# Sink keys and values in place of spent slots, merged casts and a new plan for all instructions, in a fused attention and SwiGLU kernel

## Chip, core and metric

The kernel runs on one core of a Trainium2 chip. The metric is the device time of one launch in microseconds (us), the median of several runs. A core has TensorE (PE, matmuls; PEld is its loading of weights), VectorE (DVE), ScalarE (ACT), GpSimd (POOL) and SyncE (SP, which here issues the DMA transfers). PE writes to PSUM banks; the other engines take results from there to SBUF.

## The reference, cut to what matters

Attention over 4 batches, 8 heads, 768 positions, head size 64, followed by a SwiGLU block on 3072 tokens of 512 features with 1536 inner features. Heads 0, 2 and 6 ("retrieval" heads) see all earlier positions. The other five ("streaming" heads) see the first four positions (the sinks) and the last 64.

```python
def _attn_ref(q, k, v, is_retrieval, n_sink, window):
    scores = scale * np.matmul(q, k.transpose(0, 1, 3, 2))
    rel = pos[:, None] - pos[None, :]
    causal = rel >= 0
    is_sink = pos[None, :] < int(n_sink)                  # n_sink = 4
    in_win = (rel >= 0) & (rel < int(window))             # window = 64
    stream_keep = causal & (is_sink | in_win)
    mask = np.where(retr, causal, stream_keep)
    scores = np.where(mask, scores, -1000000000.0)
    a = np.exp(scores - np.max(scores, axis=-1, keepdims=True))
    a = a / (np.sum(a, axis=-1, keepdims=True) + 1e-09)
    return np.matmul(a, v)

def _moe_ref(x, w_gate, w_val, w_out):
    g = x @ w_gate
    silu = g * (1.0 / (1.0 + np.exp(-g)))
    return silu * (x @ w_val) @ w_out
```

All inputs and the output are float32; the kernel computes in float16 with float32 sums.

## The kernel before

The positions of a batch are cut into six tiles of 128; tile `i` of a batch has queries and keys 128 i to 128 i + 127. Two tiles make a pair (`n`), which is the unit of loading: one DMA of 512 KB each for q, k and v (called x in the plan). Four tiles make a group (`g`) of 512 tokens, for which the SwiGLU block runs once over 12 slices (`j`) of 128 inner features. Everything that the kernel does is a task in a list; a string, ORDER, gives the order of the tasks in the program (two digits of base 62 for each task number; numbers from 3700 are that many plus 3700 dummy "warm" matmuls), and a string of digits, WAYS, says for each task on which of its possible engines it runs. The tile framework adds the semaphores, so each engine goes through its tasks in the given order and waits where an operand isn't ready.

```python
RINGS = {"raw": 11, "hq": 2, "e": 6, "xb": 3, "xt": 2, "sig": 2, "sil": 3, "ahead": 3,
         "h": 2 * NJ, "osb": 2, "gv": 3, "o": 1, "sc": 1, "av": 1, "tr": 1, "queue": 4}
PAIRS = [(0, 2), (4, 6), (1, 3), (5, 7)]      # two heads share the 128 rows of kT
kT = [const.tile([128, 4, S], FH, name=f"kT{n}") for n in range(2)]         # batch b uses b % 2
k2 = [const.tile([128, 4, 4, 128], FH, name=f"k2_{n}") for n in range(2)]
vt = [const.tile([128, NT, 8, 66], FH, name=f"vt{n}") for n in range(2)]
v2 = [const.tile([128, 4, 8, 66], FH, name=f"v2_{n}") for n in range(2)]
# ... cut ...
def mask_order():
    ps = buf("tr", [128, 4, 128], FP, "mk")       # the bank that transposes use as well
    nc.tensor.matmul(ps..., perm, nat..., start=True, stop=True)
def mask_fill(x):                                  # nine DVE instructions in two tasks
    ...
# ... cut ...
def cast(n, kd, j):                                # q or k of a pair, one half of the positions
    ...                                            # float32 raw -> float16 hq (or hqz)
def castv(n, m, j):
    copy(T_v[n, m][j], vt[b % 2][j * 64:(j + 1) * 64, 2 * pi + m, :, 0:64],
         r[m * 64:(m + 1) * 64, :, j])
# ... cut ...
def sinks_k(b):        # the sinks' keys into all four tiles of k2
    for j, ns in enumerate((NSINK - NSINK // 2, NSINK // 2)):
        copy(T_prev[b, 0][0], K2[:, :, :, j * 64:j * 64 + ns],
             T[:, :, j * 64:j * 64 + ns].unsqueeze(2).to_broadcast([128, 4, 4, ns]))
def sinks_v(b, m):     # the sinks' values into tile m - 1 of v2
    for j, ns in enumerate((NSINK - NSINK // 2, NSINK // 2)):
        copy(T_prev[b, 0][m], V2[j * 64:j * 64 + ns, m - 1], V[j * 64:j * 64 + ns, 0])
def previous_k(b, m):  # the last 64 keys of tile m
    copy(T_prev[b, m][0], K2[:, :, m - 1]...[:, :, :, 32:64], T[...][:, :, :, 32:64])
def previous_v(b, m):  # the last 64 values of tile m
    for r in (32, 96):
        copy(T_prev[b, m][1], V2[r:r + 32, m - 1], V[r:r + 32, m])
# ... cut ...
def block(t, p, kt):   # keys for a score matmul; kt < 0 means "sinks and the tile before"
    if kt < 0 and i > 1:
        return k2[b % 2][:, p, i - 2, :]
    kt = max(kt, 0)
    return kT[b % 2][:, p, kt * 128:(kt + 1) * 128]
def value(t, h, kt):
    if kt < 0 and i > 1:
        return v2[b % 2][:, i - 2, h, 0:65]
    return vt[b % 2][:, max(kt, 0), h, 0:65]
# ... cut ...
def gate(g, j, c, wsb, d):          # "gate" with wg_sb and "vals" with wv_sb: 4 matmuls each
    for kk in range(4):
        nc.tensor.matmul(ps, wsb[:, kk, j * 128:(j + 1) * 128], xt[:, kk, c[0]:c[1]], ...)
def outproj(g, tt, third):          # 4 matmuls of 512 columns; three of them for 128 tokens
    for j in range(third * 4, third * 4 + 4):
        nc.tensor.matmul(o_open[g, tt], hs[g, j][:, tt * 128:(tt + 1) * 128], wo_sb[:, j, :], ...)
```

A streaming head thus needs for tile `i` its own keys and a second tile of 128 slots, in which the four sinks and the last 64 keys of tile `i - 1` lie; the slots between are zero and masked. For `i` = 1 the tile before holds the sinks itself, so it is used as it is. Within a tile the positions are laid out as 64 even ones and then 64 odd ones, so the last 64 are slots 32 to 63 and 96 to 127.

Of the kernel before, what the change touches and what calls it, by code (L numbers as in the profile page):

```python
# [7 lines left out]
FP = mybir.dt.float32  # L8
# [8 lines left out]
    "000B010A0C0E0D0G0I030F050K2H0604xq070H2I090O2J2K020Jy52U2G080S2M2O2L2Vxu2P0L2W2Q2z0M2R2N3t0P302S"  # L17
    "0U312T3u32yQ2X0T372Y2Z383C0N2a392b2j1w0Q3D2l2k2e3E2m2f0Vxj2n5U2c0Y2d1x212p2g2o2r3A2q0R3B0m35342s"
    "xs2u2h2v3F3o3r2t2w0Z2i3p0c2x332y3G0n22xoBK10BU1y1z3H3PBL3I363qBM0d0oBN253JBXBVBO3Q3KBW115V3LxlBe"
    "3M0q3sBoBY3R3b0pBf0WBpBh28Bg3S3TBqBr3U3V3N0r230s3Oxi3W5QBs5S3X3Y5T0XBi3Z0u3d3a3eBP3c0tBZ5PBQBj0a"  # L20
    "3i5RBR3mBaBS3fBb0v3hBk3n0gBc3g24Bl3j4cBT3wBmBd4d0bBtBn0eBy4P3kBu3v4QC33l0hBzBv0i3x4SC0BwC40f4XBx"
    "3y0y27C1C50j4RC63z4Y1240C22BC80z41C7162ACDC9134Z43CA424514CI46CE174aCJ2DCF18CB44CK20154BCCCN0k4C"
    "4b26CG19CO4D0w2C4ECS0lCH4F1ACcCPCT0x4G4H4eCL2F1CCU29CQ4ICM1B1ECX2ECR4JCY4g4K1DCV4W4U1GCZ4V4TCdCW"
    "4h1FCa5C1I4f474iCb4j5D1H48Ce4k1K4LCf4m4l5E1JCiCg4n5H4M5K5I5J4q5L4oCj1L4p1M5G5M4w5F494r4xCkCh601O"
    "6F1N4sCl4z4A4yCoCm501P5N4t676252641Q5OCp65Cn1S5653514u1RCq6H574v54Cr4N1U66551TCuCs616q5863Cv5X1V"
    "5W591W6s4O5Y6t6v5ACw5Z5B6ECt1YD06r1X5a6u5bD1D57hCx6A5c1ZD26C5gD66D5e5dD37P5h5f6BD8CyD77Q7S7U705m"
    "CzDA7RD471686GD95nDF7j1a69DBDD7g5o1cDCDG5i1b5pDHDK6p1eDE5qDI7T1dDNDLDJ8T6o1g5j5sDy1f8E5rDM6w5t5k"
    "DODP8F5l1hDU8IDQ8JDS8HDRDV8G6x6I6yDZ6JDW5uDTDeDa6z8Q5v8VDXDbDf6L6KDj6MDg7O5w8O8RDk6ODYDc6PDlDh5x"
    "6NDdDo1i8PDi5y1kDpDt7N1j1m5z6QDmDuDq6RDv8UDr1lDn1o6YDw6ZDs1nDz1qDx6a6SE06T1p1s6bE16U6cE46V1rE26e"
    "6W6f6i6XE56j1t7Z6d6g94E67X9f6hE3E7727a6k957Y8S7iEA9i6l989p739k6mEB966n7B9j9hEM997CECE89q74A17E75"  # L30
    "ED7D9gE9EP7V7F76EG979r7W77EN9zEH78EO7HERAlEQ8DEI7IES8M9s7GEUETEJ7J7dA0EE8NEW7e7K7bEVEbAkEF79EX7f"
    "EZEYEc7c7A7LEeEdEaEg8C7M9EElEhEf7kEmEiEj7lEnEo9F8KEkEq7m8L1uEvErEp9G7sEsEwEt1vEx92F0Eu93F57tF19H"
    "EK7nF2F6Ey7oF7ELAYF3EzAa7pFAAW9yAgAX7qAZF87rFBF47yAn7uFCFDAb7zAhAiFFF98081FEFGFI827vFKFH7wAjFJ86"
    "FL83Am7x84FM879A85FN8W889C9B8XFQ898Z9DFR8Y8A8aFSFO8B9e8gFT8c8hFW9dFPFUFi8bFVFn8dFsFjFk8eFX8f8mFt"
    "8iFoFl8j8nFpFY8kFmFqFZFu8l8pFaFrFv8qFxFb8oFwFcFy8sFzG28r8tG7G3G0G88uG98w9l8vFdG18x9IFeG49n9m9J8y"
    "Ff9K9R9oGC9SFg8zG5GD9TFh90GAGEG6GH91GBAVAUGMGI9UGJGN9XAeGg9V9YGOGFAcAf9WGKGG9Z9t9w9uGPAdGL9aGh9v"
    "9xGQ9bGR9LGWGS9c9MGT9NGbGX9OGUGYGc9PGdGZGV9QA2GaGeA3H4GfA4A5H5GiA6H6AAH9GjABA7GkA8GmHAA9HBH7GlAC"
    "H8GnADAGAEGoAHHCGpAIAFAJGqGsAKHDAOGrGtALAPAMGuHEANGvHJGwHFGyHGHKGxHOHLAoHPHHApHQHMHIHTHNAQHUHRAR"
    "HVArASGzAsHSHWATAtH0HXAuAqHYAvH1AyHdHZAzH2HaAwI2AxHeH3B4HfB0B5HbB1B6B7B2HiB8HcBEB3HnHjBFB9HkBAHo"
    "HgBBHpHlHhBCHmI3BDBGHqBHHsBIHrHxHtBJHvHuHyI0HzHwIQI1IVIRITISIWIYIXIUI4IZIaI5IfI6IbIdIcIgI7IiIhIe"  # L40
    "I8IjIkIpIlIuImIqInIrIvIsIwIoIxItI9IyIzIAJ0J4J1IBJ9J5ICJOJ6JAJ2JBIDJ7J3JEJ8JJJFJCJGJKJHJLJDJMJIJP"
    "JNJQJRJUJSIEJVJTIFJWIGJXJaJYIHJbJZIIIKIJJcILJdJgJeIMJfJhINIOJiJjIPJkJl"
)
WAYS = (
    "000010000000000000000000000000000000000000000000000000000000000000000000000000000000000000000000"
    "000000000000000000000000211000010000000010111000001010011000000000000000000000000001000000200010"
    "000000010000000000000000000000011001101000001110110010010000000000100100100000000000000110110010"
    "110000010000000001001001000000000010001001000011001000010010000000000000000000000001100000200000"
    "000100001000000000000000000100000000010010011000000100100000000000000000012000022000000101001010"
    "001001000000000000010000000010002021000000000011001001000000000000000100000000000000010200000000"  # L50
    "001000000000001000000221011000000000011100100100100000000000001000000000002000021200000000101100"
    "100000000000000010000000000000000000000000000000000000000000000000000000000000000000000000000000"
    "000000000000000000000001000000000001000000000000000000000000000000000000000000000000000000000000"
    "000001000000000001000001000000000000000000000000000000000000000000000000000000000000000001000000"
    "000000000000000000000000000000000000000000000000000000000000000000000000000000000000000001000001"
    "000000000000000000000000000000000000000000000000000000000000000000000001000001000001000000000000"
    "00000000000000000000000000000000000000000000000000000100000100000100000000"
# [4 lines left out]
class Task:  # L62
# [3 lines left out]

    def __init__(self, name, ways, pos, run, deps=(), takes=(), kind="", after=(), grp=None):  # L70
        self.name, self.ways, self.pos, self.run = name, ways, pos, run
        self.deps, self.takes, self.kind = list(deps), list(takes), kind
        self.after = [x for x in after if x]
        self.grp = grp or name
        self.way = None


class Plan:
# [3 lines left out]

    INTO, BACK = 0.096, 0.120

    def __init__(self, rings):
        self.tasks = []
        self.rings = rings  # L90
        self.users = {}

    def add(self, *a, **k):
        t = Task(*a, **k)
        self.tasks.append(t)
        return t

# [4 lines left out]
    def order(self):  # L102
        n = len(self.tasks)
        numbers = [DIGITS.index(ORDER[2 * i]) * 62 + DIGITS.index(ORDER[2 * i + 1])
                   for i in range(len(ORDER) // 2)]
        assert sorted(x for x in numbers if x < 3700) == list(range(n)) and len(WAYS) == n
        for t, w in zip(self.tasks, WAYS):
            t.way = t.ways[int(w)]
        return numbers
# [3 lines left out]
def kernel(  # L113
# [22 lines left out]
    assert 0 < NSINK <= 64 and 0 < WIN <= 64  # L136
# [15 lines left out]
    QUARTERS = 0  # L152
# [9 lines left out]
    RINGS = {"raw": 11, "hq": 2, "e": 6, "xb": 3, "xt": 2, "sig": 2, "sil": 3, "ahead": 3,  # L162
             "h": 2 * NJ, "osb": 2, "gv": 3, "o": 1, "sc": 1, "av": 1, "tr": 1, "queue": 4}
# [17 lines left out]
    def copy(task, dst, src):  # L181
        if task.way[0] == "ACT":
            nc.scalar.copy(out=dst, in_=src)  # L183
        else:
            ENG[task.way[0]].tensor_copy(out=dst, in_=src)  # L185


    def act(n):
        return ("ACT", 0.083 + n * 0.000833, 0.225 + n * 0.000833, 0)

    def dve(d):
        return ("DVE", d - 0.05, d + 0.05, 0)

    def both(d):

        return ("DVE", d + 0.4, d + 0.45, 1)

    def pool(d):
        return ("POOL", d - 0.04, d + 0.06, 0)

    def pe(d):
        return ("PE", d, d + 0.22, 0)
# [32 lines left out]
    def make_masks():  # L235
        def keep(n, base, qstep, kstep):
            nc.gpsimd.affine_select(
                out=nat[:, n], in_=nat[:, n], compare_op=ALU.is_ge, fill=OFF, base=base,
                pattern=[[qstep, 2], [2 * qstep, 64]], channel_multiplier=kstep)

        nc.gpsimd.memset(perm, 0.0)
# [7 lines left out]
        keep(BAND0, 0, 1, -1)  # L249
        keep(OWN, WIN - 1, -1, 1)  # L250
# [7 lines left out]
    def mask_order():  # L258
        ps = buf("tr", [128, 4, 128], FP, "mk")
# [22 lines left out]
    k2 = [const.tile([128, 4, 4, 128], FH, name=f"k2_{n}") for n in range(2)]  # L282
    vt = [const.tile([128, NT, 8, 66], FH, name=f"vt{n}") for n in range(2)]
    v2 = [const.tile([128, 4, 8, 66], FH, name=f"v2_{n}") for n in range(2)]
# [10 lines left out]
    def fill2(x):  # L295
        ENG[T_fill2[x].way[0]].memset((k2[0], v2[0], k2[1], v2[1])[x], 0.0)

    warm_ps = []

    def warm(n=40):  # L300
# [3 lines left out]
        for _ in range(n):  # L304
            nc.tensor.matmul(warm_ps[0][:, 0:128], ident, ident, start=True, stop=True)

    T_masks = P.add("masks", [("POOL", 8.1, 8.1, 0)], -9.0, make_masks)
    T_fill0 = P.add("fill", [("DVE", 6.1, 6.1, 0)], -9.1, fill)
    T_fill1 = P.add("fill1", [("POOL", 0.35, 0.4, 0)], -8.9, fill1, after=[T_masks])
    T_fill2 = [P.add(f"fill2{x}", [dve(0.95), pool(1.7)], -0.5, (lambda x=x: fill2(x)),  # L310
                     after=[T_fill0]) for x in range(4)]
    T_mord = P.add("mord", [pe(0.216)], -0.5, mask_order, deps=[T_masks], takes=["tr"])
    T_fill = [P.add(f"mfill{x}", [dve(1.3 + 0.1 * x)], -0.4, (lambda x=x: mask_fill(x)),
# [28 lines left out]
    def whole(n):  # L342
        return [(kd, n) for kd in "qkx"]
# [698 lines left out]
```

The softmax here doesn't subtract the row's maximum and nothing guards it: scores larger than these inputs give would overflow.

## Time and profile before

| | |
|---|---|
| time, median of 3 (lowest, highest) | 268.44 us (268.37, 268.48) |
| span of the profiled execution | 266.5 us |
| instructions | 5265 |
| read from HBM, written | 28.31 MB, 6.29 MB |
| copies into v2 and k2, on POOL | 36 x 0.62 us, 7 x 0.40 us |
| copies into v2 and k2, on ACT | 28 x 0.63 us, 9 x 0.41 us, 8 x 0.22 us |
| casts of q and k to hq | ACT 28, DVE 5, POOL 1, of 512 elements |
| exponentials (e<-sc) | 71 on ACT, 62.2 us |
| tanh (sig<-gv) | 76 on ACT, 43.3 us |
| loads | 54 of 512 KB, all issued by SP |

How to read the lines: a row of digits gives the busy share in tenths for 40 equal slices of the span. A line of a group gives the line of the program, engine and operation, output and inputs by name with shape and type, how often (x), then busy us in all and mean ns of one, then the idle time of the engine just before and what ended it. The chain of waits is followed back from the last instruction to whatever released each step; "DMA" in it is the time from the issue of a transfer to its landing. An instruction in the timeline has its start, its length, and the idle time before it in brackets.

### The profile page before, as it was taken

What the parts mean: (1) busy time and instruction counts of PE and PEld (TensorE: products, weight loads), DVE (VectorE), ACT (ScalarE), POOL (GpSimd) and SP (SyncE); (2) the same over time, 40 slices, a digit from 0 to 9 for tenths busy, and PEclk for the clock granted to TensorE, in tenths of its full rate; (3) what the DMA queues carried; (4) which work ended last, traced back from release to release, by engine and by line L of the source; (5) the groups of instructions that cost most, each with busy time, mean ns of one, the idle gap of its engine ahead of it and who ended that gap; (6) DMA issues with size and microseconds to landing.
All of it is one profiled execution on the core that took longest, in us unless ns stands there. A gap on an engine that the chain in (4) does not pass through costs nothing.

```text
span 266.5 us, 5265 instructions
## 1 busy us (share of the span) xinstructions
PE 254.4 (95%) x1984; PEld 146.4 (55%) x1984; DVE 171.6 (64%) x345; ACT 171.0 (64%) x283; POOL 92.3 (35%) x126
## 2 busy tenths in 40 slices
PE   7899689999999999999999999999999999999993
PEld 7777565566555555654555555545555654444441
DVE  7665678867476886549876455578446767466332
ACT  3799999999999874895696555665443643423000
POOL 8748866445358323388003230520122020000000
PEclk9999999999999999999999999999999999999999
DMA  7999999999899939956543911551231200101134
GB/s 189 305 333 333 305 328 383 317 246 305 259 292 217 230 85 299 213 108 127 118 92 60 159 39 43 117 100 23 63 76 21 57 7 17 39 2 41 39 89 109
DMA packets 75193, 41.23 MB, mean 155 GB/s; under 512 B 27552, under 2 KB 70560, under 8 KB 75168
## 3 DMA queue, kind: packets, MB, share of 16 engines
q1 hardware_dynamic: 75088, 40.78, 61.6%
q8 instruction: 15, 0.25, 0.4%
q10 hardware_dynamic: 80, 0.13, 0.2%
q14 instruction: 10, 0.08, 0.1%
HBM read 28.31 MB, written 6.29 MB: 130 GB/s over the span
## 4 chain that ended last, share of the span: by engine, by line
PE 71%; ACT 17%; DMA 3%; SPq 3%; issue 2%; DVE 1%; ACTq 0%
PE gv L875 40%; PE o_ps L904 20%; PE sc L594 7%; ACT e L604 5%; ACT v L183 4%; PE av L624 4%; DMA raw<-in_v_dram 3%; ACT vt L183 2%; ACT hq L183 2%; SPq L330 2%; ACT sig L881 2%; SPq L338 1%; ACT k L183 1%; PE tr L472 1%; ACT wo_sb L183 0%
## 5 line engine op out<-in xcount | busy, mean ns | idle before, releaser
L604 ACT ACTIVATE e<-sc 128x1024 f16<-128x1024 f32 (+4 forms) x71 | 62.2, 880 | 26.3 <-PE sc L594 25.9
L875 PE MATMUL gv<-xt,wv_sb 128*128 128x512 f16 (+1 forms) x304 | 70.8, 368 | 1.3 <-DVE sil L885 1.3
L904 PE MATMUL o_ps<-wo_sb,h 128*128 128x512 f16 x288 | 71.2, 379 | 0.1
L875 PE MATMUL gv<-xt,wg_sb 128*128 128x512 f16 (+1 forms) x304 | 70.6, 368 | 0.6 <-DVE xt L185 0.5
L885 DVE SCALAR_TENSOR_TENSOR sil<-sig,gv 128x512 f32<-128x512 f32 (+1 forms) x76 | 49.7, 656 | 31.7 <-ACT sig L881 31.1
L881 ACT ACTIVATE sig<-gv 128x512 f32<-128x512 f32 (+1 forms) x76 | 43.3, 574 | 36.5 <-PE gv L875 36.2
L892 DVE SCALAR_TENSOR_TENSOR h<-sil,gv 128x512 f16<-128x512 f32 (+1 forms) x76 | 48.7, 654 | 7.7 <-PE gv L875 7.0
L612 POOL TENSOR_TENSOR e<-e,m 128x640 f16<-128x640 f16 (+1 forms) x16 | 27.5, 1716 | 69.4 <-ACT e L604 54.3
L875 PEld LDWEIGHTS <-wv_sb 128*128 128x128 f16 x304 | 28.9, 98 | 29.0 <-issue 2.0
L875 PEld LDWEIGHTS <-wg_sb 128*128 128x128 f16 x304 | 28.9, 98 | 27.9 <-issue 1.6
L904 PEld LDWEIGHTS <-h 128*128 128x128 f16 x288 | 26.8, 98 | 26.1 <-issue 0.5
L594 PE MATMUL sc<-qT,kT 128*128 128x256 f16 (+1 forms) x228 | 35.6, 257 | 1.3 <-ACT e L604 1.2
L594 PEld LDWEIGHTS <-kT 128*128 128x128 f16 x228 | 20.5, 98 | 12.8 <-issue 2.3
L624 PEld LDWEIGHTS <-e 128*128 128x128 f16 x472 | 20.1, 97 | 8.2 <-ACT e L604 0.9
L185 POOL COPY v<-vt 32x528 f16<-32x528 f16 (+1 forms) x36 | 22.4, 621 | 4.6 <-ACT vt L183 2.5
L185 POOL CAST vt<-raw 64x512 f16<-64x512 f32 x23 | 15.8, 689 | 20.9 <-DMA raw<-in_v_dram 16.3
L624 PE MATMUL av<-vt,e 128*128 128x65 f16 x392 | 21.8, 193 | 0.5 <-ACT e L604 0.4
L641 DVE TENSOR_TENSOR xb<-av,rc 128x256 f16<-128x256 f32 x47 | 19.8, 424 | 1.6
L629 DVE RECIPROCAL rc<-av 128x4 f32<-128x4 f32 x48 | 8.5, 178 | 19.0 <-PE av L624 18.7
L183 ACT CAST hq<-raw 128x512 f16<-128x512 f32 x28 | 16.9, 617 | 4.4 <-DMA raw<-in_q_dram 3.6
L185 DVE COPY o_sb<-o_ps 128x512 f32<-128x512 f32 x14 | 9.6, 688 | 14.4 <-PE o_ps L904 14.4
L612 DVE TENSOR_TENSOR e<-e,m 128x1024 f16<-128x1024 f16 (+1 forms) x22 | 14.7, 670 | 6.3 <-ACT e L604 6.2
(62 smaller groups left out, 193.7 us busy)
## 6 DMA issues: line engine op xcount, KB each, us to landing
raw<-in_q_dram SPq DMA_DIRECT2D x12, 512.0 KB, 7.1
raw<-in_k_dram SPq DMA_DIRECT2D x12, 512.0 KB, 7.0
raw<-in_v_dram SPq DMA_DIRECT2D x12, 512.0 KB, 6.6
out_dram<-o_sb SPq DMA_DIRECT2D x47, 128.0 KB, 2.4
raw<-in_moe_w_gate_dram SPq DMA_DIRECT2D x6, 512.0 KB, 7.8
raw<-in_moe_w_val_dram SPq DMA_DIRECT2D x6, 512.0 KB, 8.4
raw<-in_moe_w_out_dram SPq DMA_DIRECT2D x6, 512.0 KB, 8.6
kT<-hq SPq DMA_TRANSPOSE x16, 2.4
```

Source lines behind the costliest of these rows:

```text
L183: nc.scalar.copy(out=dst, in_=src)
L185: ENG[task.way[0]].tensor_copy(out=dst, in_=src)
L594: nc.tensor.matmul(sc[c // 4][:, c % 4:c % 4 + n, :], weights, moving, start=first, stop=last)
L604: nc.scalar.activation(out=e[:, 0:n], in_=whole_sc.pop((t, u))[:, 0:n], func=AF.Exp, scale=scale)
L612: ENG[task().way[0]].tensor_tensor(out=ev, in0=ev, in1=mm, op=ALU.mult)
L624: nc.tensor.matmul(av[:, n, 0:65], ee, vv, start=(m == 0), stop=(m == len(bl) - 1))
L641: nc.vector.tensor_tensor(out=xbs[t][:, :, odd, :], in0=av[:, :, 0:64], in1=rc.to_broadcast([128, 4, 64]), op=ALU.mult)
L875: nc.tensor.matmul(ps, wsb[:, kk, j * 128:(j + 1) * 128], xt[:, kk, c[0]:c[1]], start=(kk == 0), stop=(kk == 3))
L881: nc.scalar.activation(out=sg[g, j, c], in_=gs[g, j, c], func=AF.Tanh, scale=0.5)
L885: nc.vector.scalar_tensor_tensor(out=sl[g, j, c], in0=sg.pop((g, j, c)), scalar=1.0, op0=ALU.add, in1=gs.pop((g, j, c)), op1=ALU.mult)
L892: nc.vector.scalar_tensor_tensor(out=hs[g, j][:, c[0]:c[1]], in0=sl.pop((g, j, c)), scalar=0.5, op0=ALU.mult, in1=vs.pop((g, j, c)), op1=A ...
L904: nc.tensor.matmul(o_open[g, tt], hs[g, j][:, tt * 128:(tt + 1) * 128], wo_sb[:, j, :], start=(j == 0), stop=(j == NJ - 1))
```

## The change

The second tiles are given up. A streaming head never needs the first 64 keys of tile `m` again once tile `m` itself is done, so the sinks' keys and values are written over four of these spent slots in kT and vt, and tile `m + 1` then uses slot `m` of kT and vt directly. Retrieval heads still need the old contents, so only the rows of streaming heads are written: in kT they are the last two pairs and half of the second; in vt the heads are put in another sequence so that the five streaming ones lie together. The copies of 64 keys and values, the zero fills of k2 and v2 and the tiles themselves go. The write must come after the scores (or values) of tile `m` and before those of tile `m + 1`.

```diff
-    k2 = [const.tile([128, 4, 4, 128], FH, name=f"k2_{n}") for n in range(2)]
-    v2 = [const.tile([128, 4, 8, 66], FH, name=f"v2_{n}") for n in range(2)]
+    def slot(h):
+        return 1 + 2 * (h // 4) - h // 2 % 2 + 4 * (h % 2)
+    STREAMS = slice(min(slot(h) for h in range(8) if not RETR[h]), 8)
 ...
-    def sinks_k(b):
 ...
+    def sinks_k(b, m):
+        T = kT[b % 2].rearrange("c p (t j n) -> c p t j n", j=2, n=64)
+        for cs, ps in ((slice(0, 128), slice(2, 4)), (slice(0, 64), slice(1, 2))):
+            copy(T_sk[b, m], T[cs, ps, m, :, 0:NSINK // 2], T[cs, ps, 0, :, 0:NSINK // 2])
     def sinks_v(b, m):
 ...
-    def previous_k(b, m):
 ...
-    def previous_v(b, m):
 ...
+        V = vt[b % 2]
+        for j in range(2):
+            rows = slice(j * 64, j * 64 + NSINK // 2)
+            copy(T_sv[b, m], V[rows, m, STREAMS], V[rows, 0, STREAMS])
 ...
     def block(t, p, kt):
-        if kt < 0 and i > 1:
-            return k2[b % 2][:, p, i - 2, :]
-        kt = max(kt, 0)
+        kt = i - 1 if kt < 0 else kt
         return kT[b % 2][:, p, kt * 128:(kt + 1) * 128]
     def value(t, h, kt):
-        if kt < 0 and i > 1:
-            return v2[b % 2][:, i - 2, h, 0:65]
-        return vt[b % 2][:, max(kt, 0), h, 0:65]
+        kt = i - 1 if kt < 0 else kt
+        return vt[b % 2][:, kt, slot(h), 0:65]
 ...
+        if 1 <= i < NT - 1:
+            T_sk[b, i] = P.add(f"sk{b}.{i}", ["DVE", "POOL", "ACT"], ..., deps=own)
+            T_sv[b, i] = P.add(f"sv{b}.{i}", ["DVE", "POOL", "ACT"], ..., deps=T_v_of[b, i])
```

The casts of q and k: from pair 2 on one instruction casts a whole k or q to hq; where q goes to hqz (pairs 5 and up), two instructions instead of four. Casts may now run on any of the three engines.

```diff
-        for w, kd in enumerate("qk"):
-            for j in range(2):
-                ways = [act(512), both(0.5)] + ([pool(0.85)] if n < 2 else [])
+        for kd in "qk":
+            free = xqk and kd == "q"
+            for x in range(2) if n < 2 or free else [None]:
+                c = T_c[n, kd, x] = P.add(f"c{kd}{n}.{x}", ["ACT", "DVE", "POOL"], ...)
```

The masks: their construction on POOL is cut in two, of which tile 0 needs only the first; they are put in order through another PSUM bank, so that the transposes needn't wait for the fills.

```diff
-        ps = buf("tr", [128, 4, 128], FP, "mk")
+        ps = buf("o", [128, 4, 128], FP, "mk")
```

More raw buffers, and no limit of four transfers in flight in the plan:

```diff
-    RINGS = {"raw": 11, "hq": 2, ..., "ahead": 3, ..., "queue": 4}
+    RINGS = {"raw": 14, "hq": 2, ...}
```

And ORDER and WAYS are new from end to end: the order of all loads, matmuls and evacuations, and the engine of every cast, copy, mask and evacuation. The durations that the list of tasks held for planning are gone from the program; they had no part in its running. What PE, the exponentials and the SwiGLU block compute is as before, and the loads and stores move the same bytes.

## The prediction

> **What bounds the kernel now.** I read the shares by engine and the 40 slices first, then the table by stage (0 to 80 us apart from the rest), then ACT's groups between 20 and 80 us, the chain of waits, and the first 20 us of the timeline.
>
> From the page (the slices are 6.66 us each):
>
> ```profile
> PE 254.4 (95%) x1984; PEld 146.4 (55%) x1984; DVE 171.6 (64%) x345; ACT 171.0 (64%) x283; POOL 92.3 (35%) x126
> ...
> PE   7899689999999999999999999999999999999993
> ...
> ACT  3799999999999874895696555665443643423000
> ...
> PEclk9999999999999999999999999999999999999999
> DMA  7999999999899939956543911551231200101134
> ```
>
> PE seems full, but this is overlapped time. Its true work I add up from the paces in the chain: 36 gate matmuls of 512 columns in 7.77 us (0.216 each), 17 value matmuls in 0.51 (0.030), 8 transposes of 128 columns in 0.45 (0.056); 256 columns I take as 0.109. Then 544 wide and 64 half gate and value matmuls are 124.5, the output projection 288 x 0.216 = 62.2, scores with their mask matmuls 28.1, attention values 472 x 0.030 = 14.2, 152 transposes 8.5, the mask order 0.2: 237.7 us without warm-up matmuls. By stage:
>
> ```profile
> 20.00:40.00 20.00, 16.71 (x168) 12.69 (x169) 12.82 (x34) 19.58 (x39) 15.72 (x22) 1.00 1.11 322
> 40.00:60.00 20.00, 19.59 (x152) 11.22 (x151) 15.57 (x29) 19.10 (x28) 10.88 (x11) 1.00 1.05 315
> 60.00:80.00 20.00, 18.96 (x189) 11.89 (x187) 12.57 (x29) 19.45 (x32) 9.31 (x14) 1.00 1.06 285
> 80.00:140.00 60.00, 59.86 (x449) 32.85 (x447) 44.56 (x89) 45.99 (x80) 26.15 (x33) 1.00 0.76 165
> 140.00:262.00 122.00, 121.78 (x791) 62.31 (x788) 71.79 (x133) 52.70 (x80) 16.77 (x17) 1.00 0.28 56
> ```
>
> Columns: PE, PEld, DVE, ACT and POOL busy with counts, clock, DMA share, GB/s. Before 80 us run 144 gate and value, 48 projection, 115 score, 150 attention-value matmuls and 127 transposes: at the same paces 24.2 + 10.4 + 10.8 + 4.5 + 7.1 = 57 us of work. So 23 us are lost there, and after 80 us about one (180.7 of work in 182). Only the first 80 us can give anything. There ACT is busy 58.1 of 60 us from 20 to 80, and the DMA engines are full until about 60. ACT in that stretch:
>
> ```profile
> L183 ACT CAST hq<-raw 128x512 f16<-128x512 f32 x14 | 8.5, 617 | 0.1
> ...
> L183 ACT COPY v<-vt 32x528 f16<-32x528 f16 x8 | 5.0, 629 | 0.2
> L183 ACT COPY v<-vt 2x528 f16<-2x528 f16 x8 | 5.0, 624 | 0.1
> ...
> L183 ACT COPY k<-kT 128x256 f16<-128x256 f16 x2 | 0.8, 416 | 0.0
> ```
>
> The chain goes through the same groups until 77 us and then through PE:
>
> ```profile
> 9.41 9.03 DMA raw<-in_v_dram
> ...
> 64.30 0.64 ACT v L183
> 64.95 0.63 ACT v L183
> ...
> 76.32 0.49 ACT sig L881
> 76.82 0.92 ACT e L604
> 78.10 1.73 PE gv L875 x8
> ```
>
> And at the start DVE fills the masks for 2.94 us while PE waits for the bank that they hold; the first scores come at 12.66:
>
> ```profile
> 6.65 2.94 DVE L270 TENSOR_SCALAR m<-mk 128x512 f16<-128x512 f32 x9
> ...
> 9.64 0.62 PE L472 MATMUL tr<-ident,hq 128*128 128x128 f16 x8 [0.41 <-DVE m L270]
> ...
> 12.66 0.38 PE L594 MATMUL sc<-nat,perm 128*128 128x512 f16 x1
> ```
>
> **What the Trainium skill says.** "Perfetto Trace Analysis", Identifying the Most-Contended Engine, calls matmul busy time a bad measure because matmuls are pipelined: the trace agrees, 254.4 busy against 237.7 of work. "VectorE: DVE Perf Modes", The TRN2 errata — SBUF-src ops pay a fixed extra latency per instruction, says that an operation with its source in SBUF pays a fixed cost per instruction on VectorE and ScalarE: ACT's cast takes 617 ns for 512 elements and 1056 for 1024, so 178 ns are fixed, and the copy of 2 partitions costs as much as that of 32 (624, 629). "SBUF — State Buffer", Who interferes with whom, says that a VectorE copy or cast in a two-port mode shuts GpSimd out for the whole instruction; POOL's vt casts average 689 ns against 610 for its hq cast, which agrees but doesn't show the cause. "TensorE: Matmul & The Clock Gate", What's actually happening, says that an idle window of about 3.4 us halves the clock; the trace stays at 1.00 up to 260 us, so it shows no such fall.
>
> **The change, part by part.**
>
> *Second tiles.* Removed: 64 copies of 528 elements (36 on POOL 22.4 us, 28 on ACT 17.5), 16 of 256 for keys (ACT 3.7, POOL 2.8), 8 small ones (1.3), and four memsets (DVE 2.7, POOL 1.8): 52 us of engine time. In their place the diff has 16 key and 16 value tasks of two small instructions each. The digits of WAYS, read against the numbering of the tasks, give 2 + 2 of these tasks to ACT, 6 + 4 to DVE, 8 + 10 to POOL. A value copy has 330 elements instead of 528; scaled I take 0.45 us on ACT or POOL, 0.2 on DVE, and 0.2 for a key copy. That is 32 x 0.2 + 24 x 0.45 + 8 x 0.2 = about 19 us, most of it on POOL.
>
> *Casts.* Query and key casts of pairs 2 and up become one instruction (1024 elements) instead of two. In WAYS 12 of those 13 are POOL's (about 1.05 us each, as its 128x1024 weight cast at 1038 ns) and ACT keeps four of 512. ACT loses 24 x 617 ns = 14.8 us; POOL gains 12.6, less than it lost in copies.
>
> *Sum for ACT*: -17.5 - 5.0 - 14.8 and smaller shifts (six more output copies +3.5, three more evacuations +2, sink copies +2.7, fewer value and query casts -3): about -32 in added durations; consecutive ones overlap by some 0.1 us, so some -28 busy. Between 20 and 80 us, 8.5 + 10.0 + 1.1 = 19.6 of the 58.1 fall away. ACT then no longer sets the pace. DVE gains six weight casts (some 5 us) and loses memsets; its 64% become some 67%.
>
> *Start.* The mask order moves to another bank and the fills behind the first evacuations; k1 and q1 come sooner and x1 is the 7th load instead of the 8th. First scores at about 9.5 to 10 instead of 12.66: up to 3 us, if the loads let PE keep it.
>
> *Warm-up matmuls.* 125 fillers become 31: 94 x 0.056 = 5.3 us less, but they stood in idle time, so nothing of its own.
>
> **What is then the bound.** I went along the new order of PE and added the work that remains behind each matmul that needs a load. x1 lands at 18.44 now as the 8th; a load of 0.524 MB at 322 GB/s is 1.63 us; as the 7th it lands at 16.8. The last gate weights g5 are 25th: 16.8 + 18 x 1.63 = 46.1, with cast and wait 47.2. Behind their first use (gate 10 of group 0) lie 62 gate, 65 value and 72 projection tasks of four matmuls, the scores and values of the later tiles, in all 201.9 us: PE can't end before 249.1. For v1 (13th, 27.7, 220.9 behind it) it is 248.6, for v3 (29th, 54.0, 194.8 behind) 248.8. The plan leans on the loads with no slack from 25 to 54 us. PE ended at 262.05, so at most 13 us are to be had. I add 1.5 us for what PE lost after 80 us now, and 2 us for stalls where the new order meets late operands: PE's end 252.5. The last evacuation and store took 266.5 - 262.0 = 4.5; the median time stood 1.9 over the span: 252.5 + 4.5 + 1.9 = 258.9. I chose 258.5.
>
> **The rivals.**
> 1. *The in-place write becomes the wait.* Scores of tile i, then the sink copy, then scores of i+1, and the same for values: 16 tiles at about 1 us, if all are exposed, would give 16 us back (about 270). For it: POOL does most of them, and a mask of 2.1 us can stand before one. Against it: the order has PE work between the two, such as 2.6 us between the values of tiles 4 and 5. I expect under 2 us.
> 2. *The loads slip.* SP issues everything in order, so a store or transpose that waits holds back the loads behind it; with no slack each us costs a us. It costs 2 to 5 us: 261 to 264. For it: the transposes of q5 stand ahead of the loads of pairs 6 and up, and wait for casts; against it: 14 raw buffers instead of 11.
> 3. *POOL or DVE is the bound*, by the twelve casts on POOL and two-port casts on DVE beside them: POOL busy 35.9 of 60 us now from 20 to 80, so only bursts can hurt; 1 to 4 us.
> 4. *The clock halves* in the thinner start without fillers: some 3 us. Against it: PE's longest wait in the trace of before is 1.4 us.
> 5. *Nothing was lost to ACT*, DMA alone held the first 80 us: then only the order of loads and the start pay, 3 to 5 us, about 264.
>
> **Range and chances.** The floor is 249.1 + 6.4 = 255.5, perhaps 1 less if loads run at their best rate; rivals 2 and 3 together reach 264. Range 254.5 to 264. Faster by 2% means under 263.1: 0.82. Within: 0.14, slower (rival 1 in full, or several together): 0.04.
>
> **What would show it.** Right: no copies into second tiles; ACT some 140 to 147 us busy and under 85% between 20 and 80 us; first scores before 10.5; PE with some 67 us of work by 80 us; the chain to 55 us through DMA and casts, then PE; clock at 1.00. Wrong: waits of PE scores or values for the sink copies of several us in all, POOL above 90% between 20 and 60, or loads landing later than above.

## The result and the profile after

| | before | after |
|---|---|---|
| time, median (lowest, highest) | 268.41 us (268.37, 268.48) | 264.62 us (263.69, 264.90) |
| ratio to before, with its interval | 1 | 0.985 (0.984 to 0.987) |
| span of the profiled execution | 266.5 us | 262.8 us |
| instructions | 5265 | 4993 |

The change makes the kernel 1.5% faster, 3.8 us. The prediction was 9.9 us, and 264.62 us lies just above its range. Busy times and slices of the page of after (40 slices of 6.57 us):

```profile
PE 247.6 (94%) x1890; PEld 141.3 (54%) x1890; DVE 174.6 (66%) x357; ACT 140.3 (53%) x216; POOL 89.7 (34%) x123
...
PE   7878899899999989999899999999999999999993
...
DVE  3887988989777569857398747527459365557421
ACT  2777797686548467758286754722363522323100
...
PEclk9999999999999999999999999999999999999998
DMA  6999999994999979794972342253212221211143
```

ACT's row has no run of nines any more; its 171.0 us became 140.3. DVE's row has eights and nines (one seven) from slice 2 to slice 10, that is to 66 us. The table by stage shows the same (PE, PEld, DVE, ACT and POOL busy with counts, clock, DMA share, GB/s):

```profile
20.00:40.00 20.00, 18.00 (x204) 14.43 (x205) 17.34 (x41) 16.27 (x26) 14.94 (x21) 1.00 1.12 320
40.00:60.00 20.00, 18.14 (x189) 11.37 (x187) 17.79 (x37) 14.38 (x22) 13.33 (x18) 1.00 1.09 335
60.00:80.00 20.00, 20.00 (x140) 10.93 (x138) 16.18 (x33) 12.01 (x17) 8.44 (x10) 1.00 0.91 208
```

From 20 to 60 us DVE is busy 35.1 of 40 us (28.4 before) and ACT 30.7 (38.7 before). The two have changed places.

**Where the time went.** Busy PE hides what PE did, so I counted work: each matmul of the trace by its columns, at the pace of 36 matmuls of 512 columns in 7.77 us, warm-up matmuls as nothing. That is 235.3 us for either kernel. The rest of the time up to a moment is lost there (cumulative us):

| up to (us) | 20 | 40 | 60 | 80 | 140 | last matmul | which ends at |
|---|---|---|---|---|---|---|---|
| before | 13.8 | 20.3 | 21.2 | 23.4 | 24.7 | 26.7 | 262.0 |
| after | 12.3 | 15.8 | 18.6 | 18.8 | 22.1 | 23.0 | 258.3 |

The change wins 1.5 us by 20 us and 3.0 more by 40, gives 1.9 back by 60, wins 2.0 by 80, gives 2.0 back by 140 and wins 1.1 at the end. The predicted floor (PE's end at 249.1 us, set by the loads) is a loss of 13.8 us in this count. At 24 us after had lost about that. Then it lost 4.9 more up to 66 us, 3.4 from there to 140 and 0.9 to the end.

The start went as planned. The timeline of after shows DVE filling the masks behind two of the evacuations, while PE goes on with scores:

```profile
9.26 2.93 DVE L248 TENSOR_SCALAR m<-mk 128x128 f16<-128x128 f32 x9
9.40 0.39 PE L530 MATMUL sc<-qT,kT 128*128 128x128 f16 x3 [0.86 <-DVE kT L177]
```

The chain of waits of after was to go through DMA and casts up to 55 us and then through PE. From 18 to 56 us it is on PE for 14.8 us, on DVE for 10.8, on ACT for 6.6 and on POOL for 3.8; from 57 to 63 us it is on DVE. From 66 to 93 us, where the prediction had PE alone, it is on DMA for 17.7 us: loads that stood behind the transposes of q5, and then a transpose of q. Pieces of it (start, length, what):

```profile
27.50 0.60 DVE wv_sb L177
28.10 1.80 DVE e L548
29.90 0.34 DVE sil L771
...
49.09 0.60 DVE sil L771
49.69 0.60 DVE kT L177
...
50.84 0.60 DVE wg_sb L177
51.44 0.60 DVE h L778
...
66.54 6.17 DMA raw<-in_q_dram
...
74.41 7.43 DMA raw<-in_k_dram
...
89.09 4.11 DMA qT<-hqz
```

DVE goes through its instructions in the order of the program, so a gate weight that lies ready in its raw buffer waits for whatever stands ahead of it. The last gate weights g5 landed at 46.92 us (46.1 predicted); their cast is that of 50.84 (it starts at 50.75, while the instruction before it ends), and the first matmul with them ran at 51.52 (47.2 predicted). Its neighbours v1 and v3 landed at 26.48 and 53.57 us (26.6 and 52.7 by the prediction's pace). So the transfers kept the predicted times and the operands did not.

Two instructions of DVE are far longer than their like, a mask on this chain and a cast beside it. The timeline of after at 27 us and at 46 us, cut to these and what follows:

```profile
27.52 1.83 POOL L548 TENSOR_TENSOR e<-e,m 128x640 f16<-128x640 f16 x1 [1.22 <-ACT e L540]
...
28.02 1.89 DVE L548 TENSOR_TENSOR e<-e,m 128x1024 f16<-128x1024 f16 x1
...
29.82 0.74 DVE L771 SCALAR_TENSOR_TENSOR sil<-sig,gv 128x256 f32<-128x256 f32 x2
...
30.29 0.60 PE L761 MATMUL gv<-xt,wv_sb 128*128 128x256 f16 x4 [0.99 <-DVE sil L771]
```

```profile
46.24 1.03 POOL L177 CAST hq<-raw 128x1024 f16<-128x1024 f32 x1
...
46.31 1.50 DVE L177 CAST wv_sb<-raw 128x1024 f16<-128x1024 f32 x1
...
50.75 0.68 DVE L177 CAST wg_sb<-raw 128x1024 f16<-128x1024 f32 x1
...
51.52 0.81 PE L761 MATMUL gv<-xt,wg_sb 128*128 128x512 f16 x3
```

The cast at 46.31 takes 1.50 us, a cast of the same shape at 50.75 takes 0.68. In both cases of a long DVE instruction a POOL instruction had started 0.07 to 0.50 us earlier, and DVE's ended 0.54 to 0.56 us after POOL's end (29.35 and 47.27), as if it had only then begun. PE's wait of 0.99 us at 30.29 follows on the first one (experiment 8 tests it).

### The profile page after: what moved, and what is told of

Same layout as the page of the kernel before. It is cut to its first block, busy times and chain, and to the rows that moved or that the text cites. A ratio compares the mean times of both kernels' runs of the same rounds, so it can differ in the third digit from the quotient of the medians.

```text
span 262.8 us, 4993 instructions
## 1 busy us (share of the span) xinstructions
PE 247.6 (94%) x1890; PEld 141.3 (54%) x1890; DVE 174.6 (66%) x357; ACT 140.3 (53%) x216; POOL 89.7 (34%) x123
## 4 chain that ended last, share of the span: by engine, by line
PE 67%; DMA 12%; DVE 6%; SPq 6%; POOL 3%; ACT 3%; issue 2%; POOLq 0%; DVEq 0%; ACTq 0%
PE gv L761 36%; PE o_ps L790 20%; PE sc L530 6%; DMA raw<-in_q_dram 6%; PE av L560 4%; DMA qT<-hqz 3%; DMA raw<-in_k_dram 3%; SPq L309 3%; SPq L400 2%; DVE sil L771 1%; DVE e L548 1%; ACT e L540 1%; POOL hq L177 1%; DVE h L778 1%; POOL e L548 1%
## 5 line engine op out<-in xcount | busy, mean ns | idle before, releaser
L761 PE MATMUL gv<-xt,wv_sb 128*128 128x512 f16 (+1 forms) x304 | 73.0, 368 | 1.0 <-DVE sil L771 1.0
L761 PE MATMUL gv<-xt,wg_sb 128*128 128x512 f16 (+1 forms) x304 | 72.9, 368 | 0.6 <-POOL wg_sb L177 0.6
L778 DVE SCALAR_TENSOR_TENSOR h<-sil,gv 128x512 f16<-128x512 f32 (+1 forms) x76 | 49.3, 656 | 24.2 <-PE gv L761 23.0
L548 POOL TENSOR_TENSOR e<-e,m 128x1024 f16<-128x1024 f16 (+1 forms) x17 | 31.8, 1873 | 54.1 <-ACT e L540 54.0
L761 PEld LDWEIGHTS <-wv_sb 128*128 128x128 f16 x304 | 28.6, 98 | 28.0 <-issue 1.3
L530 PEld LDWEIGHTS <-kT 128*128 128x128 f16 x276 | 24.6, 98 | 15.7 <-DMA qT<-hqz 3.0
L177 POOL CAST vt<-raw 64x512 f16<-64x512 f32 x21 | 13.8, 660 | 11.1 <-DMA raw<-in_v_dram 10.3
L177 POOL CAST hq<-raw 128x1024 f16<-128x1024 f32 (+1 forms) x14 | 14.8, 1058 | 6.6 <-DMA raw<-in_q_dram 5.1
L548 DVE TENSOR_TENSOR e<-e,m 128x640 f16<-128x640 f16 (+1 forms) x21 | 15.8, 754 | 1.8 <-ACT e L540 1.7
L175 ACT COPY o_sb<-o_ps 128x512 f32<-128x512 f32 x15 | 8.8, 584 | 11.6 <-PE o_ps L790 11.6
L177 POOL COPY vt<-vt 2x330 f16<-2x330 f16 x20 | 9.6, 481 | 14.2 <-PE av L560 13.6
L177 DVE COPY o_sb<-o_ps 128x512 f32<-128x512 f32 x8 | 5.5, 690 | 9.3 <-PE o_ps L790 8.0
```

Source lines behind the costliest of these rows:

```text
L177: ENG[task.way].tensor_copy(out=dst, in_=src)
L530: nc.tensor.matmul(sc[c // 4][:, c % 4:c % 4 + n, :], weights, moving, start=first, stop=last)
L548: ENG[task().way].tensor_tensor(out=ev, in0=ev, in1=mm, op=ALU.mult)
L778: nc.vector.scalar_tensor_tensor(out=hs[g, j][:, c[0]:c[1]], in0=sl.pop((g, j, c)), scalar=0.5, op0=ALU.mult, in1=vs.pop((g, j, c)), op1=A ...
```

## The experiments

The names of tasks in the diffs: `wc` cast of weights (g gate, v value, o output, with the number of the load), `cx`, `ck`, `cq` casts of x (the v input), k and q of a pair, `evk`, `evq` evacuations of transposed k and q, `mask`, `ex` and `sk` mask, exponential and sink-key copy of a tile, `dq` transposes of q by DMA. Most edits change only a task's engine, by a dictionary that overrides WAYS, or its place in ORDER.

**1. Fewer casts on DVE.** Eight casts go from DVE to ACT.

```diff
+    MOVED = {"wc v1": "ACT", "wc g4": "ACT", "wc v2": "ACT", "cx3.0.1": "ACT",
+             "wc g5": "ACT", "cx4.1.0": "ACT", "ck6.None": "ACT", "cq5.0": "ACT"}
-            t.way = t.ways[int(w)]
+            t.way = self.MOVED.get(t.name, t.ways[int(w)])
```

> Eight casts (weights v1, g4, v2, g5; half a v of pairs 3 and 4; k of pair 6 and half of q of pair 5) go from VectorE to ScalarE; nothing else moves. Theory A (VectorE sets the pace from 27 to 65 us): some 6 us leave its queue there and the q5 cast no longer comes at 62.7 us, so the time falls by 2.5 to 5 us, to 259.5 to 262. Theory B (only the hole in the loads from 54 to 63 us costs): 1 to 2 us less, as much as the run that moves four loads ahead of that wait. Theory C (loads alone bound the first 60 us): no change, 264 to 265.

Measured: 263.15 us, ratio 0.980 (0.978 to 0.981), 1.5 us better than after: less than theory A gave, and in B's range. DVE's busy time from 20 to 60 us fell to 32.6, ACT's rose to 36.1. PE's loss by 60 us stayed at 18.5: ACT takes about half as long again for a cast, and PE now waits 3.0 us for ACT (0.2 in after). The gain came between 60 and 140 us. There PE's wait for q transposes by DMA nearly goes away, first in after and then in this kernel (us in total, times, longest):

```profile
PE sc L530 <- DMA qT<-hqz: 2.0, 2, 1.2
```

```profile
PE sc L531 <- DMA qT<-hqz: 0.3, 1, 0.3
```

SP issued the first transpose of q5 at 62.42 us instead of 63.24. So relief of DVE pays here by way of SP's order, not by operands that came sooner in the first 60 us.

**2. Loads ahead of the waiting transposes.** SP stood 8.7 us in front of the transposes of q5, whose cast came late on DVE, and the loads behind them stood too.

```diff
+        for name in ['load q6', 'load q8', 'load x9', 'load x5']:
+            numbers.remove(at(name))
+            numbers.insert(numbers.index(at("dq5.0")), at(name))
```

> Four loads (q6, q8, x9, x5) stand ahead of the transpose of q5 in SP's order, so that its wait of 8.7 us no longer holds them back. Theory A (VectorE sets the pace to 65 us, the late q transposes cost only the two waits at 92 and 127 us): 1 to 2 us less, 262.5 to 263.5. Theory B (the hole in the loads is the main loss against the prediction): 3 to 5 us less. Neither: no change, if the transposes that follow only queue behind more loads.

Measured: 265.73 us, ratio 0.989 (0.988 to 0.991), 1.1 us slower than after, and none of the three forecasts. Filling the hole puts the transposes behind the loads: the first two of q5 landed at 70.18 and 72.47 us instead of 68.27 and 70.89, and PE waited 1.04 us for the second. So the hole can't be filled this way for a gain; that it costs nothing is not shown.

**3. The sink copies left out.** The kernel leaves out all copies of sinks, so its streaming heads see four old keys in their place.

```diff
-            copy(T_sk[b, m], T[cs, ps, m, :, 0:NSINK // 2], T[cs, ps, 0, :, 0:NSINK // 2])
+            pass
-            copy(T_sv[b, m], V[rows, m, STREAMS], V[rows, 0, STREAMS])
+            pass
```

> The 32 sink copies are left out, so the streaming heads see four old keys in place of the sinks. Rival 1 of the prediction (the in-place write is the wait): 4 us less or more, under 260.5. My theory: the copies cost little more than their time on VectorE in the tight stretch, under 1.5 us, 263 to 264.6.

Measured: 262.86 us, ratio 0.979 (0.977 to 0.980). All that is left of the copies, as wait and as load on the engines together, is 1.8 us, a little more than my theory had and less than half of what rival 1 needs.

**4. The kernel before without its copies.** The bodies of the four copy tasks are empty, so second tiles hold no keys or values. ORDER and WAYS are those of before.

```diff
-                copy(T_prev[b, 0][0], K2[...], T[...]...)
+                pass
-            copy(T_prev[b, m][1], V2[r:r + 32, m - 1], V[r:r + 32, m])
+            pass
```

> The kernel before with all copies into its second tiles left out (88 instructions, 48 us of ScalarE and GpSimd), order unchanged; streaming heads see zero keys there. If ScalarE set the pace from 20 to 80 us, as the prediction had it: 5 to 9 us less, 259 to 263. If the arrival of the loads in that order set it: under 2 us less, 266.5 or more.

Measured: 264.70 us, ratio 0.986 (0.985 to 0.988). The table by stage of this kernel (same columns):

```profile
20.00:40.00 20.00, 17.66 (x179) 13.71 (x179) 14.76 (x37) 15.12 (x27) 8.08 (x9) 1.00 1.11 325
40.00:60.00 20.00, 20.00 (x168) 11.74 (x165) 14.46 (x28) 18.12 (x26) 10.99 (x12) 1.00 1.10 329
60.00:80.00 20.00, 18.23 (x175) 11.22 (x173) 11.73 (x28) 16.02 (x26) 6.37 (x8) 1.00 1.00 255
```

The copies were 48 us of ACT and POOL (36 x 0.62 + 28 x 0.63 = 40 us of value copies, 8 of key copies). Without them ACT is busy 49.3 of 60 us instead of 58.1, and the time falls by 3.7 us, between the two forecasts and as much as by the whole change. So the copies were on the path before, on ACT or on POOL (the run frees both and doesn't tell them apart), but the next limit stood only some 4 us behind them, in the old order as well.

**5 to 7. Added load, one engine at a time.** The kernel after with instructions nobody waits for, ahead of named tasks between 25 and 62 us: eight DVE memsets of 592 ns (4.7 us), eight ACT copies of 618 ns (4.9 us), six POOL memsets of 944 ns (5.7 us).

```diff
+            if P.tasks[number].name in ['wc v1', 'evk3.0', 'wc g4', 'sk0.4', 'mask6.0',
+                                        'wc v2', 'wc g5', 'sv1.1']:
+                nc.vector.memset(idle, 0.0)
```

(5; in 6 `nc.scalar.copy` ahead of eight exponentials, in 7 `nc.gpsimd.memset` ahead of six casts and copies.)

> Eight fills of an unused tile (640 float32 each, some 0.6 us by the trace's 0.49 for 512) are added to VectorE between 27 and 63 us, 4.8 us in all, on which nothing waits. If VectorE's queue sets the pace there: 3 to 5 us more than the changed kernel (264.6). If the loads do: under 1 us more.

> Eight copies of 512 elements into an unused tile (0.5 to 0.6 us each, 4.4 in all) are added to ScalarE between 24 and 55 us. ScalarE has some 9 us free between 20 and 60 in the changed kernel. If it is off the path: under 1 us more. If all three elementwise engines are bound together, since each waits for the others: 2 to 4 us more.

> Six fills of an unused tile (1024 float16, some 0.9 us each, 5.4 in all) are added to GpSimd between 24 and 50 us. GpSimd has 12 us free between 20 and 60. Off the path: under 1 us more. If its queue, or its hold on the port that it shares with VectorE, is on the path: 2 to 5 us more.

Measured, against after's 264.62 us:

| | time | ratio to before | cost | per us added |
|---|---|---|---|---|
| 5, DVE + 4.7 us | 268.79 | 1.0015 (0.9999 to 1.0030) | 4.2 us | 0.9 |
| 6, ACT + 4.9 us | 266.27 | 0.991 (0.988 to 0.994) | 1.7 us | 0.3 |
| 7, POOL + 5.7 us | 266.38 | 0.992 (0.990 to 0.993) | 1.8 us | 0.3 |

A microsecond added to DVE costs nearly a microsecond of the kernel, three times what it costs on the others, which lie between their two forecasts. PE's waits in run 5 (what it waited for: us in total, times, longest):

```profile
PE gv L762 <- DVE sil L772: 2.1, 3, 1.0
PE gv L762 <- DVE h L779: 2.1, 1, 2.1
PE xtr L594 <- DVE xb L578: 1.5, 2, 0.7
```

The added memsets did not draw out POOL's work (28.6 us busy from 20 to 60, 28.3 in after), and PE's loss grew where they stand, by 5 us up to 66 us. But they also shifted what runs beside what. I added up, for DVE's instructions that start between 24 and 66 us, what each took beyond the shortest of its shape, where that is 0.15 us or more: 3.3 us in after, 4.7 in run 5, 4.8 in run 6, 4.6 in run 7. Every one of them began while a POOL instruction was running. So in run 5 DVE's queue grew by some 6 us and not 4.7, which makes 0.7 us of time for each; and in 6 and 7 the 1.5 and 1.3 us that DVE lost may be most of the cost. These two runs don't show that ACT or POOL themselves were on the path.

**8. One mask moved.** The only edit puts the POOL mask of 27.52 us on DVE, the engine that has too much to do already.

```diff
+    MOVED = {"mask4.1": "DVE"}
```

> The mask of tile 4 that ran on GpSimd from 27.5 to 29.4 us goes to VectorE, in front of or behind its neighbour there. If VectorE's mask took 1.89 us because GpSimd held the shared port: it now takes some 0.7, the two together 1.2 to 1.3, and VectorE is free 0.6 us sooner though it has an instruction more. If the 1.89 us is of its own (its form): 2.4 us for the two. In the time at most 1 us.

Measured: 263.09 us, ratio 0.980 (0.978 to 0.982), 1.5 us better than after, from two runs (262.7 and 263.5, both below the lowest of after); at most 1 us was expected. DVE's timeline in this kernel:

```profile
28.02 0.69 DVE L549 TENSOR_TENSOR e<-e,m 128x1024 f16<-128x1024 f16 x1
...
29.81 0.48 DVE L549 TENSOR_TENSOR e<-e,m 128x640 f16<-128x640 f16 x1
```

From 26.4 us up to the first of these DVE's timeline is as in after. Both masks on DVE take 0.69 + 0.48 = 1.17 us of it, as expected if POOL held the other one back; that one beside POOL's took 1.89. Giving DVE work unloaded it, by 0.7 us; the rest of the 1.5 us isn't traced, and POOL was relieved of 1.83 us as well.

**9. A mix.** Six of the casts of experiment 1 to ACT, two casts to POOL, and to DVE one evacuation and that mask.

```diff
+    MOVED = {"wc g4": "ACT", "wc v2": "ACT", "wc g5": "ACT", "cx4.1.0": "ACT",
+             "ck6.None": "ACT", "cq5.0": "ACT", "cx3.0.1": "POOL", "cx2.1.1": "POOL",
+             "evk4.0": "DVE", "mask4.1": "DVE"}
```

> VectorE is relieved again, but not all on ScalarE, which stood at 90% in the run with eight casts: weights g4, v2, g5, half a v of pair 4, k of pair 6 and half of q of pair 5 to ScalarE; two half v of pairs 3 and 2 to GpSimd; k evacuation of pair 4 and one mask of tile 4 to VectorE. If the three engines together are the bound and balance is what counts: 260.5 to 262.5. If in the run before the gain came only from the earlier q of pair 5: 263.2 as there.

Measured: 262.37 us, ratio 0.977 (0.976 to 0.979), the best of all kernels here. Its table by stage:

```profile
20.00:40.00 20.00, 18.24 (x206) 14.45 (x207) 16.55 (x43) 17.55 (x28) 13.67 (x21) 1.00 1.13 318
40.00:60.00 20.00, 19.23 (x192) 11.98 (x190) 16.19 (x34) 16.44 (x25) 13.39 (x20) 1.00 1.06 332
```

DVE and ACT now carry the same (32.7 and 34.0 of 40 us). PE's loss by 60 us is 17.5 instead of 18.6, at the end 20.3 instead of 23.0. The time is what balance was to give, but the mix has experiment 8's mask in it, DVE's excess beside POOL between 24 and 66 us is 0.8 instead of 3.3 us, and PE's wait for q transposes 0.2 instead of 2.0, so balance is not shown to be the reason. PE's end, 255.6 us, still stands 6.5 us above the predicted floor.

**10. Later loads.** Two loads of output weights go ahead of the load of q3, so that those behind it come later; their casts (2 us on ACT) are moved too. (Two loads more of 512 KB were to test this first; that kernel has no time, since its two buffers found no room in SBUF.)

```diff
+        for name in ['load o5', 'load o0']:
+            numbers.remove(at(name))
+            numbers.insert(numbers.index(at("load q3")), at(name))
```

> Two loads that are needed late (output weights o5 and o0) go ahead of the load of q3, so that q3 and the 17 loads behind it land some 3.1 us later, with the same bytes in all; their two casts run early on ScalarE (2 us). If the loads set the end with no slack: 3 us more or above, 267.5 or more. If VectorE's queue is later than the loads by now: 0.5 to 2 us more.

Measured: 267.48 us, ratio 0.997 (0.995 to 0.998), 2.9 us slower than after, between the two forecasts. v1 landed 2.9 us later than in after, g5 and v3 2.5. Not all of the cost is the lateness. Windows of the profiled run, in which the third number from the end is PE's clock:

```profile
28.00:30.00 2.00, 0.62 (x8) 0.45 (x8) 0.59 (x1) 2.00 (x5) 2.00 (x4) 1.00 1.19 297
30.00:32.00 2.00, 1.00 (x5) 0.74 (x6) 2.00 (x4) 1.05 (x2) 1.16 (x2) 0.65 1.13 306
32.00:34.00 2.00, 2.00 (x13) 1.46 (x11) 1.05 (x3) 0.81 (x1) 1.36 (x3) 0.50 1.02 333
```

PE waited for a cast from 27.99 to 28.84 and for a weight cast from 29.46 to 31.00, and then worked until 34.0 at half clock, which loses half of these 3.0 us. Of the 20 runs 13 have a mean clock of at most 0.991 and a median of 267.54 us, five have at least 0.996 and a median of 266.69. So without the fall of the clock the edit costs about 2.1 us, of which the 2 us on ACT may be 0.7 by the slope of experiment 6: per us of lateness some 0.5 to 0.8. Loads are close to the path; they are not all of it.

**11. The cast of q5 alone to ACT.** It tests whether experiment 1 gained by letting SP go on sooner.

```diff
+    MOVED = {"cq5.0": "ACT"}
```

> Of the eight moved casts only one: half of q of pair 5 goes from VectorE, where it ended at 63 us, to ScalarE. SP's wait of 8.7 us before the transpose of q5 falls to 2 or 3 us, and all that follows in SP's order comes sooner. If that was the gain of the run with eight casts: 263 to 263.5. If VectorE's relief was: 264 to 264.8.

Measured: 264.78 us, ratio 0.986 (0.985 to 0.988), the same as after. SP's waits, first of after and then of this kernel:

```profile
SPq L400 <- DVE hqz L177: 9.7, 2, 8.7
```

```profile
SPq L401 <- ACT hqz L176: 12.8, 3, 8.8
```

The edit missed its aim: ACT's queue reaches the cast as late as DVE's (62.3 us), so SP waits as long and issues the transpose at 62.98 us instead of 63.24. The run shows that this cast by itself gains nothing. It doesn't test what an earlier transpose is worth: in experiments 1 and 9, where the whole queue ahead was shorter, the transpose came at 62.42 and 61.56 us.

**12. More work away from POOL.** The mix of experiment 9 without one of its casts, and with two more masks or evacuations and a sink copy on DVE, to have fewer instructions of the two engines side by side.

```diff
-             ... "cx2.1.1": "POOL", ...
+             ... "mask5.0": "DVE", "evq2.00": "DVE", "sk1.2": "DVE"}
```

> The mixed assignment again, with one half v of pair 2 back on ScalarE, and three tasks more on VectorE: the mask of tile 5 that holds the port on GpSimd from 35.8 to 38.4 us, the first q evacuation of pair 2 (its neighbour waits 1.1 us for ScalarE on the same bank), and a sink copy that PE waited 0.6 us for on ScalarE. If what counts is fewer holds of the shared port and shorter waits at these places: 0.5 to 1.5 us under the mixed run, 261 to 262. If VectorE's queue is full again by 1.5 us: 262.5 to 263.5.

Measured: 263.97 us (262.7 to 265.9), ratio 0.984 (0.981 to 0.988), 1.6 us slower than experiment 9 and outside both forecasts. DVE is at 17.15 + 17.80 = 35.0 of 40 us again, and PE's waits show it:

```profile
PE av L561 <- DVE xb L578: 2.3, 4, 1.2
PE sc L531 <- DVE kT L178: 2.3, 3, 1.2
```

In experiment 9 these two are 0.6 and 1.1. The overlap was not avoided either: DVE's excess beside POOL, counted as in 5 to 7, is 1.8 us here and 0.8 in experiment 9.

## Why the prediction was wrong

**Right.** ACT's busy time (140.3; 140 to 147 predicted) and its share between 20 and 80 us (42.7 of 60, 71%; under 85%); DVE's 66% (67%); first scores at 9.40 (before 10.5); the landings, within a microsecond; the tail (262.8 - 258.3 = 4.5 us) and the 1.8 us between span and median. Rival 4 didn't come (clock 1.00 in every stage up to 260 us), though experiment 10 shows that it was near. Rival 1 cost at most 1.8 us (under 2; experiment 3). Rival 5 named the time that came, about 264, but not for its reason: it had nothing lost to the copies, and experiment 4 finds 3.7 us there.

**The step that failed** is "What is then the bound": that with ACT relieved the loads alone set PE's end, 249.1, plus 1.5 and 2 us. The working went from a landing straight to a matmul, with one cast of 1.1 us between. For g5 these 1.1 us became 4.6 (46.92 to 51.52), while its other two terms held: the landing was 0.8 us late, and 202.2 us of work lay behind the first use (201.9 predicted). The operand waited in an in-order queue, and from 27 to 65 us this was DVE's, with 2.2 us of gaps in all. In PE's loss: 13.8 + 3.5 = 17.3 us predicted, 23.0 measured (18.7 of them by 66 us, 22.1 by 140). The 5.7 us between are the whole error against the 258.9 us that the sum gave (264.62 - 258.9). Three things go into it; the runs don't divide it among them:

1. *DVE took ACT's place.* DVE's average of 67% was predicted right and read wrongly. It is 35.1 of 40 us exactly in the stretch in which the plan leans on the loads. Experiment 5 measures what added work there costs, 0.7 to 0.9 us per us. Experiments 1 and 9 take work off and get 1.5 and 2.3 us back, but next to nothing and 1.1 us of PE's loss were gone by 60 us: the rest came where PE waited for q transposes, which in after stood behind a cast late in DVE's queue (rival 2, below).
2. *Rival 3 was sized as bursts of 1 to 4 us and left out of the sum*, whose 2 us for stalls stand for all rivals. To take one mask from beside another was worth 1.5 us, 0.7 of them as DVE's own time (experiment 8). Between 15 and 66 us nine DVE instructions were 0.15 us or more longer than the shortest of their shapes, 4.6 us in all, each begun while a POOL instruction was running. The trace of before has four of them, 1.6 us, with two masks of 1.09 and 1.21 us instead of 0.67: it was there to be seen. From 24 to 66 us this excess is 3.3 us in after, 2.1, 2.1, 0.8 and 1.8 in the kernels that are faster than after by other assignments (experiments 1, 8, 9, 12), 3.8 and 3.9 in 2 and 11, which are not faster, and 4.6 to 4.8 in 5 to 7; experiments 3 and 10, which change the copies and the loads, have 4.2 and 3.4. That is one execution of each. The excess goes largely together with the time, but only experiment 8 comes near to isolating it. I quoted the Trainium skill for one direction only, that DVE shuts POOL out. The same section of "SBUF — State Buffer", Who interferes with whom, says that the engine which issues first gets the shared ports for the whole instruction, and that a VectorE instruction with two SBUF inputs contends with GpSimd's reads. The trace agrees: POOL first by 0.50 us, and DVE's mask took 1.89 instead of 0.69 us. By moving twelve whole casts to POOL and six weight casts to DVE the change put the two engines with shared ports side by side.
3. *The loads are near the path too.* Later loads cost 0.5 to 0.8 us per us. (Added work on ACT and POOL cost 0.3 each, but that may be DVE's longer instructions again.) With DVE's 0.7 to 0.9 the loads make more than one, which a single chain can't give; I read it as several chains within some microseconds of each other, each of which an addition of some microseconds makes the longest.

**Also off.** The work of PE: 237.7 by the paces in the chain, 235.3 by columns, so before had lost 26.7 us and not 24, and 3.3 of them after 80 us, where the prediction saw about one and added 1.5; after loses 4.2 there. "67 us of work by 80" was 61.2. The start was worth 1.5 us by 20 us and not up to 3: between 9.4 and 20 us PE waited another 2.0 us, mostly for DVE's evacuations and casts. In the bound, 54.0 for v3 should be 53.8, which changes nothing. Of the predicted sum for copies, 52 us of engine time removed was right, but its worth was 3.7 us (experiment 4).

**Open.** Rival 2 came true in part. SP stood 8.7 us at the transposes of q5, the loads behind them landed late (no load landed between 62.5 and 69.9 us), and the chain that ended last goes through them. Of the 3.4 us lost from 66 to 140, 2.0 are PE's two waits for q transposes by DMA; in experiments 1 and 9, where these are 0.3 and 0.2, only 1.6 and 1.7 us are lost there. But no run moves the transposes alone: experiment 2 put them later, and experiment 11 moved them by 0.3 us. How much DVE's load and the overlap each take of the 4.9 us lost from 24 to 66 isn't separated. What makes the runs of experiment 12 spread by 3.2 us stays open as well.

## What to carry to other kernels

When a full engine is relieved, look for the next limit stage by stage and with its queue, not by average: an engine at 66% over the kernel can be at 88% just where the operands arrive, and an in-order queue adds its wait between landing and use. Idle instructions put into one engine's queue measure cheaply what a microsecond there costs, if one also looks at what they shift: here such work on ACT or POOL made DVE's instructions 1.3 to 1.5 us longer. Before work is moved between VectorE and GpSimd, look at what runs beside it on the other: a mask on the busier engine can cost less than one beside it. And an issue that stands in SP's order behind a cast inherits that cast's delay, with every load behind it.

## What was not expected of the hardware

The length of a DVE instruction beside a POOL one: a mask of 128x1024 took 1.89 us instead of 0.69, a cast 1.50 instead of 0.68, and each ended some 0.55 us after POOL's end. It goes the other way as well: POOL's weight cast at 39.61 us, begun 0.06 us after a DVE mask, took 1.51 us instead of 1.04.

The clock fell to half for 3.4 us (30.6 to 34.0) in experiment 10 though PE was not idle throughout: before the fall it had waited 0.85 and 1.15 us (the second wait went on to 31.0), with 0.62 us of transposes between. "TensorE: Matmul & The Clock Gate", What's actually happening, in the Trainium skill speaks of an idle window of about 3.4 us; here 2.0 us of waits within 2.6 came before it.
